# Changing the row format of all loads, the matmul tiling behind them and the whole instruction order of a retention and token-mixing kernel

## The chip, the cores and the metric

One core of a Trainium2 chip runs the whole program. The metric is the device time of one execution in microseconds, median over runs. A profile of one execution stands beside it; its times count from the first instruction of the span.

## What is computed

```python
# q, k, v: [4, 8, 768, 64] float32; w_q, w_k: [512, 64]; w_out: [512, 512]
gamma = 1 - 2.0 ** (-5 - arange(8))                 # one decay per head
for t in range(768):
    state = gamma * state + outer(k[t], v[t])       # per batch and head, 64x64
    y[t] = scale * q[t] @ state
x = y, heads side by side                           # [4, 768, 512]
W_tok = scale * (x @ w_q) @ (x @ w_k).T            # per batch, 768 x 768
mixed = W_tok @ x                                   # [4, 768, 512]
out = relu(mixed) @ w_out                           # [4, 768, 512] float32
```

The kernel multiplies in the other order: z = (x w_k)^T x, a 64 x 512 matrix for each batch, is summed over the tokens; then (x w_q) z is `mixed`. So a batch's z needs all of its 768 tokens.

## The kernel before, in words

The 3072 tokens are cut into 12 **pairs** of two chunks of 128 tokens, three pairs to a batch (NP = 3); pair p has 8 heads, held as 4 head pairs of 2 x 64 columns (HP = 4). Every step of every pair is a small function. Nothing is scheduled automatically: the list ORDER names the steps one after the other, with the engine of each copy or cast (`:A` is ScalarE, shown as ACT; `:V` VectorE, DVE; `:P` GpSimd, POOL) and the PSUM bank (`@2`). Each engine works through its own instructions in that order and waits where an input is missing.

The steps of pair p: `ck`, `cq`, `cv` cast k, q, v from the float32 staging tiles `k_st`, `q_st`, `v_st` to the bfloat16 tiles `ks`, `qs`, `vs` (cv also multiplies by the decay table `fv`). `trk`, `trq` transpose ks and qs on TensorE into PSUM (the PSUM tile is called `banks`), `ek`, `eq` (or `ekq`) copy the result out (`kq`). `sc` computes scores, `eat` masks them into `at_sb`; `st` adds k^T v to the running state, `es` copies the state out (`s_sb`); `ia`, `in`, `ic` build y in PSUM from scores and state; `ex` scales y into x (`x_nat`). `xt`, `exT` transpose x; `wqk` computes x w_k and x w_q, `ew` and `ewt` evict them (`wk_n`, `wqT`); `zm` adds the pair's part of z, `ez` evicts z after the third pair; `mx` computes `mixed`, `r` is the relu, `pj` the projection by w_out, `eo` the eviction into `o_st`. `fill` multiplies a tile of zeros (`warm`), with no result used.

`load` (L151) brings each of k, q, v of a pair as 128 partitions x 8 heads x 512 bytes, one row being two neighbouring tokens. The pairs 0 to 3 (TYPES "2") work in this layout directly, with matmuls on 64 rows. The pairs 4 to 11 (TYPES "1") rearrange k and v while casting: `ck1`, `cv1` (L556) move each quarter to other partitions, four instructions of 64 partitions x 512 for each tensor. LOADS is the order of the DMAs on the SP queue; a load waits until the staging tile 18 loads earlier has been cast (STAGES). Stores (`s0`, `s11/1`) come after all loads, in 2 KB rows.

Of the kernel before, what the change touches and what calls it, by code (L numbers as in the profile page):

```python
# [17 lines left out]
ekq.0.0:A ck.1:A fill.6@6 st.0.0 cq.1:V cv.1:P cv.2:P es.0.0:A sc.0.1@0 cv.3:P eat.0.1:V mask:P  # L18
ck.4.0:P ck.2:A ck.4.1:P fill.2@6 st.0.1 cv.4.0:P sc.0.0@2 trq.1@4 cv.4.1:P trk.1@4 WO.1:P
ekq.1.1:V ekq.1.0:V es.0.1:V cq.2:A ck.5.0:P fill.1@6 ia.0.1@0 WO.0:P in.0@0 fill.2@6 sc.1.0@4  # L20
eat.0.0:V fill.4@6 sc.1.1@2 st.1.0 eat.1.0:V es.1.0:A ia.0.0@0 cv.5.0:P trk.2@4 ic.0@0 trq.2@4
st.1.1 eat.1.1:V ekq.2.0:V W:A cv.5.1:P ekq.2.1:A ex.0:V fill.3@6 sc.2.0@4 sc.2.1@2 in.1@0
eat.2.0:V ia.1.1@0 ia.1.0@0 es.1.1:A ck.6.1:P xt.0@4 st.2.0 cv.6.1:P eat.2.1:V ic.1@0 exT.0:V
ia.2.1@2 ex.1:V ia.2.0@2 ck.3:A es.2.0:A trk.3@4 ic.2@2 in.2@2 ex.2:V cv.6.0:P cv.7.0:P cq.3:A
wqk.0@6 trq.3@4 ekq.3.1:A ekq.3.0:V xt.1@0 st.3.0 exT.1:V es.3.0:A xt.2@2 cq.4:A exT.2:V cv.7.1:P
sc.3.0@4 ew.0:V sc.3.1@0 wqk.1@2 wqk.2@3 eat.3.1:V ewt.1:A ew.1:A trq.4@0 eat.3.0:V trk.4@0
ck.8.0:P ewt.2:A ew.2:A st.3.1 ic.3@2 cq.8:P cv.8.0:P cv.8.1:P in.3@2 ia.3.0@2 ia.3.1@2 ek.4:V
zm.0.0@4 ewt.0:V eq.4:A es.3.1:A ex.3:V cv.9.1:P sc.4.0@0 sc.4.1@5 st.4.0 eat.4.0:V xt.3@2 exT.3:V
eat.4.1:V es.4.0:A zm.0.1@4 ez.0:A mx.0@0 ck.5.1:A cq.5:V in.4.1@2 cv.9.0:P wqk.3@4 r.0:A ewt.3:A
ew.3:A ia.4.0@2 ia.4.1@2 in.4.0@2 trk.5@5 mx.1@0 ex.4:V st.4.1 trq.5@5 ek.5:V r.1:A eq.5:V  # L30
ck.10.1:P pj.0.1@4 eo.0.1:A pj.0.0@0 sc.5.0@5 es.4.1:V xt.4@3 sc.5.1@1 cv.10.0:P st.5.0 eo.0.0:A
pj.1.0@0 eat.5.0:V ck.6.0:A eat.5.1:V pj.1.1@5 exT.4:A es.5.0:V ia.5.0@3 ia.5.1@3 in.5.1@3
in.5.0@3 eo.1.0:A mx.2@0 eo.1.1:A ck.11.1:P cq.6:V ex.5:V wqk.4@2 ew.4:V trq.6@5 trk.6@5 eq.6:V
r.2:A xt.5@0 ek.6:V ewt.4:A pj.2.1@3 pj.2.0@2 sc.6.0@5 ck.7.1:A exT.5:V sc.6.1@0 wqk.5@4 eo.2.1:A
zm.1.0@3 cq.7:V eat.6.0:V ew.5:V eat.6.1:V st.6.0 zm.1.1@3 eo.2.0:A ck.7.0:A trk.7@5 es.6.0:A
trq.7@5 ez.1:A st.6.1 ewt.5:A eq.7:V ek.7:V mx.3@2 ia.6.1@0 ia.6.0@0 es.6.1:A st.7.0 r.3:A
in.6.1@0 es.7.0:A ex.6:V sc.7.0@5 mx.4@2 pj.3.1@4 r.4:A sc.7.1@0 eat.7.0:V pj.3.0@2 st.7.1 xt.6@5
eat.7.1:V exT.6:V ck.8.1:A eo.3.1:A pj.4.0@3 eo.3.0:A ia.7.1@1 es.7.1:A trq.8@5 cq.11:P in.7.0@1
ck.9.1:V trk.8@5 eo.4.0:A mx.5@3 in.7.1@1 eq.8:V ck.9.0:A ia.7.0@1 pj.4.1@0 r.5:A eo.4.1:A ek.8:V
sc.8.0@5 sc.8.1@3 cq.9:A st.8.0 ex.7:V es.8.0:A xt.7@1 exT.7:A pj.5.0@0 eat.8.1:V trq.9@3 trk.9@3  # L40
in.8.1@1 eo.5.0:A eat.8.0:V ek.9:V eq.9:A cv.10.1:P in.8.0@1 ia.8.1@1 cv.11.0:P ia.8.0@1 pj.5.1@0
ex.8:V wqk.6@6 xt.8@1 ew.6:V eo.5.1:A sc.9.1@3 cq.10:A exT.8:V wqk.7@0 wqk.8@1 ew.7:A zm.2.0@2
ck.10.0:A eat.9.1:V sc.9.0@3 ew.8:V ewt.6:A zm.2.1@2 st.9.0 ewt.8:A ez.2:A trk.10@5 trq.10@5
mx.6@1 eat.9.0:V es.9.0:A st.9.1 ewt.7:A in.9.1@3 r.6:A ek.10:V ia.9.0@3 ia.9.1@3 mx.7@0 eq.10:V
es.9.1:A ex.9:V ck.11.0:A r.7:A sc.10.0@5 eat.10.0:V st.10.0 pj.6.0@2 trk.11@3 trq.11@3 eq.11:V
ek.11:V eo.6.0:A sc.10.1@0 es.10.0:A xt.9@5 eat.10.1:V pj.6.1@2 in.10.0@3 cv.11.1:P in.10.1@3
exT.9:A sc.11.0@5 eo.6.1:A st.10.1 es.10.1:A eat.11.0:V wqk.9@2 ia.10.1@3 ia.10.0@3 ew.9:A ewt.9:A
sc.11.1@0 ex.10:V mx.8@5 eat.11.1:V st.11.0 r.8:A pj.7.1@2 in.11.0@3 xt.10@5 exT.10:V es.11.0:A
in.11.1@3 ia.11.0@3 ia.11.1@3 pj.8.0@0 ex.11:V wqk.10@1 eo.7.1:A xt.11@3 ewt.10:V exT.11:V ew.10:A
eo.8.0:A pj.7.0@6 wqk.11@3 ew.11:V eo.7.0:A zm.3.0@0 ewt.11:V zm.3.1@0 ez.3:A mx.11@0 r.11:A  # L50
mx.10@3 mx.9@5 pj.8.1@2 pj.11.1@0 eo.8.1:A pj.11.0@1 eo.11.1:A r.10:V r.9:A pj.10.0@2 pj.10.1@0
eo.10.0:A eo.11.0:V eo.10.1:A pj.9.1@6 eo.9.1:A pj.9.0@2 eo.9.0:A
# [5 lines left out]
q10 v10 k11 q11 v11 s0 s1 s2 s3 s4 s5 s6 s7 s8 s11/1 s11/0 s10/0 s10/1 s9/1 s9/0  # L58
""".split()

TYPES = "222211111111"
STAGES = 18
OBUFS = 11
CASTS = dict(k=6, v=6, q=4)
WBYTES = 512
OBYTES = 2048
KQS = 2
# [3 lines left out]
def kernel(  # L71
# [35 lines left out]

# [16 lines left out]
    def bank32(b, n=1):  # L124
        return banks[:, b : b + n, :].rearrange("p n f -> p (n f)")
# [4 lines left out]
    pairs = [dict() for _ in range(NG)]  # L130
    z_sbs = [None] * B
# [9 lines left out]

    def load(name, p, half=None, eng=None):
        src = {"k": k, "q": q, "v": v}[name]
        b, cp = divmod(p, NP)
        st = pairs[p]
        if name + "_st" not in st:
            st[name + "_st"] = stage_pool.tile([128, 2, HP, 2, D], FP32, name=name + "_st", tag="st")
        xs = slice(0, 2) if half is None else slice(half, half + 1)  # L150
        dma = (eng or nc.sync).dma_start(  # L151
            out=st[name + "_st"][:, xs].rearrange("g x hp j d -> g (x hp) (j d)"),
            in_=src[b, xs.start * HP : xs.stop * HP, cp * 2 * C : (cp + 1) * 2 * C, :].rearrange(
                "h (g j) d -> g h (j d)", j=2
            ),
        )
    wstages = {}

    def load_weights(token):
        w_st = stage_pool.tile([128, 2, HP, 2, D], FP32, name=token + "_st", tag="st").rearrange(  # L160
            "p x hp j d -> p (x hp j d)"
        )
        if token == "w":
            st = w_st[:, 0 : 2 * NDM * DH].rearrange("p (w a h) -> p w a h", w=2, a=NDM)
            for i, src in enumerate((moe_w_q, moe_w_k)):
                nc.sync.dma_start(out=st[:, i], in_=src.rearrange("(a p) h -> p a h", p=128))
        else:
            st = w_st.rearrange("p (a m) -> p a m", a=2)
            for i in range(2):
                a = 2 * int(token[1:]) + i  # L170
                nc.sync.dma_start(
                    out=st[:, i], in_=moe_w_out[128 * a : 128 * a + 128, :], max_dma_last_dim=WBYTES
                )
        wstages[token] = st

    def load_token(token):
        if token[0] in "wo":
            load_weights(token)
        else:
            load(token[0], int(token[1:]))  # L180

    load("k", 0, 0, nc.scalar)
    load("k", 0, 1, nc.sync)

    queue = list(LOADS)
    staged = ["k0"]
    cast = set()

    def more_loads():
        while queue:
            token = queue[0]
            if token[0] == "s":
                if not stored(token[1:]):
                    return
                queue.pop(0)
                continue
            n = len(staged)
            if n >= STAGES and staged[n - STAGES] not in cast:  # L200
                return
            staged.append(token)
            load_token(queue.pop(0))

    parts = {}

    def release(token, n):
# [8 lines left out]

    warm = const_pool.tile([128, 512], BF16, name="warm")
    nc.vector.memset(warm, 0.0)  # L218


    ln_v = const_pool.tile([128, NP, H, 2], FP32, name="ln_v")
    ln_y = const_pool.tile([128, NP * 2, H], FP32, name="ln_y")
    for h in range(H):
        ln = math.log(1.0 - 2.0 ** (-5.0 - h))
        nc.vector.memset(ln_v[:, :, h, :], -ln)
        nc.vector.memset(ln_y[:, :, h], ln)
    tv = const_pool.tile([128, NP, H, 2], FP32, name="tv")
    nc.gpsimd.iota(
# [688 lines left out]
```

## Time and profile before

| | |
|---|---|
| median of 3 runs | 101.49 us (99.64, 101.49, 101.58) |
| span of the profiled execution | 98.4 us, first to last instruction |
| busy TensorE / DVE / ACT / POOL | 85.4 / 72.4 / 64.4 / 59.8 us |
| moved by DMA | 20.19 MB read, 6.29 MB written, 26.74 MB in all queues |
| DMA rate, mean over the span | 272 GB/s |

The profiled execution has no time of its own beside the span; the median of the runs lies 3.1 us above the span, which is start and end of the program outside of it. The page cuts the span into 40 slices of 2.46 us: busy tenths of each engine, the granted TensorE clock (PEclk, 9 is full), the mean busy share of the 16 DMA engines and GB/s. Views by time list instructions with start and duration; TensorE matmuls are pipelined, so the distance from the start of one group to that of the next says what a group costs, and the duration says more than that.

### The profile page before, as it was taken

The numbers are of one execution on the slowest core, as the hardware profiler recorded it, in microseconds if no ns is written. First come the engines' busy times: TensorE is split into PE (matmuls) and PEld (weight loads), VectorE is DVE, ScalarE is ACT, GpSimd is POOL, SyncE is SP. The second block draws the span as 40 slices with busy tenths as digits, with TensorE's granted clock in tenths as the row PEclk, the third lists the DMA queues.
The fourth block names the chain that finished last, engine by engine and source line by source line (L and its number), as shares of the span: only waits on it lengthen the run. The fifth ranks groups of instructions, "written<-read, shape, count | busy, mean of one in ns | idle before, by whom it ended". The sixth has DMA issues, their size and how long they took to land. (4 is left out here: it accounts for less than half of the span.)

```text
span 98.4 us, 4214 instructions
## 1 busy us (share of the span) xinstructions
PE 85.4 (87%) x1847; PEld 54.9 (56%) x1861; DVE 72.4 (74%) x105; ACT 64.4 (65%) x110; POOL 59.8 (61%) x77
## 2 busy tenths in 40 slices
PE   4999789876697988999999999689999999989950
PEld 1334465564585775655747647357786576644410
DVE  3032489999489299979999899998899999624200
ACT  4344823928090458969799899987899955347750
POOL 4646070250989998999999999999999800000000
PEclk9999999999955699999999999999999999999999
DMA  1999998999999999999999999999998150040983
GB/s 18 291 347 347 339 343 200 308 295 309 314 335 316 301 271 286 333 320 316 315 330 318 272 307 295 336 327 341 394 401 321 37 214 9 0 191 22 388 340 125
DMA packets 43954, 26.74 MB, mean 272 GB/s; under 512 B 1952, under 2 KB 40864, under 8 KB 43936
## 3 DMA queue, kind: packets, MB, share of 16 engines
q1 hardware_dynamic: 43408, 26.22, 86.1%
q8 instruction: 14, 0.23, 0.9%
q10 hardware_dynamic: 528, 0.26, 0.9%
q14 instruction: 4, 0.03, 0.1%
HBM read 20.19 MB, written 6.29 MB: 269 GB/s over the span
## 5 line engine op out<-in xcount | busy, mean ns | idle before, releaser
L556 POOL TENSOR_TENSOR vs<-v_st,fv 64x512 bf16<-64x512 f32 x32 | 34.8, 1086 | 2.2 <-DMA v_st<-in_v_dram 0.2
L831 PE MATMUL banks<-wout_sb,relu 128*128 128x512 bf16 x85 | 21.7, 380 | 1.0 <-issue 0.6
L639 DVE TENSOR_TENSOR at_sb<-banks,cmask 128x1024 bf16<-128x1024 f32 x16 | 19.1, 1217 | 1.1 <-PE banks L627 1.1
L136 ACT CAST ks<-k_st 64x512 bf16<-64x512 f32 (+2 forms) x20 | 13.6, 682 | 5.9 <-DMA k_st<-in_k_dram 5.6
L362 POOL TENSOR_TENSOR vs<-v_st,fv 128x1024 bf16<-128x1024 f32 (+1 forms) x4 | 7.2, 1810 | 13.2 <-DMA v_st<-in_v_dram 13.2
L136 ACT COPY o_st<-banks 128x512 f32<-128x512 f32 x23 | 13.2, 587 | 2.7 <-PE banks L831 2.5
L137 DVE COPY kq<-banks 128x1024 bf16<-128x1024 bf16 x18 | 11.8, 686 | 2.5 <-PE banks L585 1.8
L831 PEld LDWEIGHTS <-relu 128*128 128x128 bf16 x96 | 8.2, 98 | 8.8 <-issue 0.4
L824 ACT ACTIVATE relu<-banks 128x1024 bf16<-128x1024 f32 x11 | 11.3, 1024 | 2.1 <-PE banks L809 1.6
L328 PE MATMUL banks<-warm 128*128 128x512 bf16 x34 | 11.0, 467 | 1.6 <-DVE warm L218 1.3
L136 ACT COPY kq<-banks 128x1024 bf16<-128x1024 bf16 x6 | 6.0, 1011 | 6.5 <-PE banks L386 4.6
L712 DVE TENSOR_TENSOR x_nat<-banks,fy 128x1024 bf16<-128x1024 f32 x8 | 9.8, 1220 | 0.6 <-PE banks L664 0.3
L429 DVE TENSOR_TENSOR at_sb<-banks,cmask 128x1024 bf16<-128x1024 f32 x8 | 9.4, 1216 | 0.4 <-PE banks L417 0.2
L137 POOL CAST ks<-k_st 64x512 bf16<-64x512 f32 x14 | 8.5, 608 | 0.8
L758 PE MATMUL banks<-xT,wqk_w 128*128 128x256 bf16 x48 | 8.1, 297 | 0.0
L136 ACT CAST qs<-q_st 128x1024 bf16<-128x1024 f32 (+1 forms) x6 | 5.9, 979 | 2.9 <-DMA q_st<-in_q_dram 2.9
L136 ACT CAST s_sb<-banks 128x256 bf16<-128x256 f32 x17 | 6.4, 377 | 1.2 <-PE banks L678 1.0
L328 PEld LDWEIGHTS <-warm 128*128 128x128 bf16 x37 | 3.7, 114 | 6.1 <-issue 3.2
L627 PE MATMUL banks<-kq 64*128 64x128 bf16 x128 | 5.9, 217 | 1.1 <-DVE kq L137 0.8
L137 DVE CAST qs<-q_st 128x1024 bf16<-128x1024 f32 (+1 forms) x5 | 4.2, 850 | 3.3 <-DMA q_st<-in_q_dram 3.3
L137 DVE COPY xT<-banks 128x1024 bf16<-128x1024 bf16 x9 | 6.2, 685 | 0.3 <-PE banks L730 0.3
L530 DVE TENSOR_TENSOR x_nat<-banks,fy 128x1024 bf16<-128x1024 f32 x4 | 4.9, 1218 | 1.7 <-PE banks L461 1.6
(78 smaller groups left out, 134.6 us busy)
## 6 DMA issues: line engine op xcount, KB each, us to landing
q_st<-in_q_dram SPq DMA_DIRECT2D x12, 512.0 KB, 6.6
v_st<-in_v_dram SPq DMA_DIRECT2D x12, 512.0 KB, 6.5
k_st<-in_k_dram SPq DMA_DIRECT2D x11, 512.0 KB, 6.4
out_dram<-o_st SPq DMA_DIRECT2D x9, 512.0 KB, 6.4
out_dram<-o_st SPq DMA_DIRECT2D x6, 256.0 KB, 2.0
o_st<-in_moe_w_out_dram SPq DMA_DIRECT2D x4, 256.0 KB, 5.2
k_st<-in_k_dram ACTq DMA_DIRECT2D x1, 256.0 KB, 4.2
k_st<-in_k_dram SPq DMA_DIRECT2D x1, 256.0 KB, 3.9
```

What stands on the lines that cost most here:

```text
L136: return nc.scalar.copy(out=out, in_=in_)
L137: return ENGINES[e].tensor_copy(out=out, in_=in_)
L328: nc.tensor.matmul(out=bank32(b), lhsT=warm[:, 0:128], rhs=warm, start=True, stop=True)
L362: ENGINES[e].tensor_tensor(out=st["vs"][:, :, :, xs].rearrange("p hp j x d -> p x (hp j) d"), in0=st["v_st"][:, xs].rearrange("p x hp j d ...
L429: ENGINES[e].tensor_tensor(out=st["at", half].rearrange("p x hi j t -> p (x hi) (j t)"), in0=st["at_ps", half].rearrange("p (n t) -> p n t ...
L556: ENGINES[e].tensor_tensor(out=st["vs"][rows(j), c].rearrange("p hp x d -> p x hp d"), in0=st["v_st"][rows(c), :, :, j], in1=fv[rows(c), p ...
L627: nc.tensor.matmul(out=ps[:, x, hi, c, :], lhsT=st["kT"][rows(x), hp, c, :], rhs=st["qT"][rows(x), hp, c, :], start=(hi == 0 and c == 0), ...
L639: ENGINES[e].tensor_tensor(out=st["at", half].rearrange("p x hi c t -> p (x hi c) t"), in0=st["at_ps", half].rearrange("p (n t) -> p n t", ...
L712: nc.vector.tensor_tensor(out=st["x"].rearrange("p x c i n -> p (x c i n)").rearrange("p (m d) -> p m d", d=D), in0=st["y_ps"].rearrange(" ...
L758: nc.tensor.matmul(out=st["wq_ps"], lhsT=wqk_sb[:, a, 0 : 2 * DH], rhs=st["xT"][:, a].rearrange("p c t -> p (c t)"), start=False, stop=(a ...
L824: nc.scalar.activation(out=dst, in_=st["mx_ps"], func=ACT.Relu)
L831: nc.tensor.matmul(out=bank32(b), lhsT=st["relu"][:, a, j, :], rhs=wout_sb[:, a, :], start=(a == 0), stop=(a == NDM - 1),)
```

## The change

All pairs get one type, "3". A k or v row is one token of one head, 256 bytes, and a partition is a token: two DMAs of 128 x 8 x 64 for each load, so that casts are one whole instruction of 128 x 1024 (`cast`). A q row is 8 neighbouring tokens, 2 KB; the transposes of q undo this order with a permuted identity, `perm`. w_out comes in 2 KB rows instead of 512 bytes. `wqk` becomes `wk` and `wq`: wq is computed for the two chunks in two column tiles (64 output rows each), and both results stand side by side in PSUM, so that `ew` evicts them in one instruction (`w_sb`). z is put on both row halves (`ez` in three parts), `mx` runs by 128 columns on the row half of its chunk, `r` is one relu of 128 x 512 for each chunk. Transposes may go to one bank, 8 of 128 x 128 (`@4`), or two banks, 16 of 64 x 64 (`@12`). The order of all steps, of loads and of stores is new, with 14 fill matmuls, all at the start, instead of 37 spread over the first third. Stage tiles are 17.

```diff
-ck.0.0:V ck.0.1:A fill.15@6 trk.0@0 cq.0.1:A cq.0.0:V fill.4@6 trq.0@0 cv.0.1:P cv.0.0:V ekq.0.1:A
...
+fill.14@6 mask.3:P ck.0.0:A ck.0.1:P cq.0:A trk.0@0 trq.0@12 ek.0:V cv.0.0:P eq.0:V sc.0.0@12
...
-q0 v0 k1 q1 v1 k2 q2 w v2 k3 q3 v3 k4 q4 v4 o0 o1 k5 q5 v5 k6 q6 v6 k7 q7 v7 k8 q8 v8 k9 q9 v9 k10
...
+k0 q0 v0 q1 k1 k2 q2 v1 w v2 k3 q3 q4 k4 v3 v4 q5 o1 o0 k5 q6 k6 v5 v6 q7 k7 v7 k8 q8 k9 q9 v8 k10
+v9 k11 q11 q10 v10 v11 s0/0 s2/1 s0/1 s1/1 s2/0 s1/0 s3/1 s4/1 s4/0 s3/0 s5/0 s5/1 s8/0 s6/1 s8/1
...
-TYPES = "222211111111"
-STAGES = 18
+TYPES = '333333333333'
+STAGES = 17
...
+            if name == "q":
+                t = st.rearrange("p (x e) -> p x e", x=2)
+                nc.sync.dma_start(
+                    out=t,
+                    in_=src.rearrange("(h x) (g j) d -> g h x (j d)", x=2, j=J),
+                )
...
+                t = st.rearrange("p (c h d) -> p c h d", c=2, h=H)
+                for c in range(2):
+                    nc.sync.dma_start(
+                        out=t[:, c], in_=src[:, c * C : (c + 1) * C].rearrange("h p d -> p h d")
+                    )
...
+    def wq(e, bs, p):
...
+        for a in range(NA):
+            for c in range(2):
+                nc.tensor.matmul(
+                    out=st["w_ps"][rows(c), 1],
+                    lhsT=wq_w[:, a, :],
+                    rhs=st["xT"][:, a, c, :],
...
+    def mx(e, bs, p):
...
+                nc.tensor.matmul(
+                    out=st["m_ps"][c][:, a * C : a * C + C],
+                    lhsT=z[rows(c), half ^ c, i * C : i * C + C],
+                    rhs=st["w"][rows(c), 1, :],
...
+    def r(e, bs, p, c):
+        st = pairs[p]
+        st["r", c] = relu_pool.tile([128, NA, C], BF16, name="relu")
```

What stands first on the SP queue before (after its half of k0; the other half is on ACT's queue): one DMA for each of k, q, v.

```order
L151 DMA k_st<-in_k_dram 128x4x128
L151 DMA q_st<-in_q_dram 128x8x128
L151 DMA v_st<-in_v_dram 128x8x128
L151 DMA k_st<-in_k_dram 128x8x128
L151 DMA q_st<-in_q_dram 128x8x128
L151 DMA v_st<-in_v_dram 128x8x128
```

What stands first there after the change, where the last number of a row counts the elements of a DMA row (64 of float32 are 256 bytes, 512 are 2 KB):

```order
L189 DMA k_st<-in_k_dram 128x8x64 x2
L177 DMA q_st<-in_q_dram 128x2x512
L189 DMA v_st<-in_v_dram 128x8x64 x2
L177 DMA q_st<-in_q_dram 128x2x512
L189 DMA k_st<-in_k_dram 128x8x64 x4
L177 DMA q_st<-in_q_dram 128x2x512
L189 DMA v_st<-in_v_dram 128x8x64 x2
L162 DMA w_st<-in_moe_w_q_dram 128x4x64
L162 DMA w_st<-in_moe_w_k_dram 128x4x64
```

Each k or v has become two DMAs, all on SP; q1 has moved ahead of k1, and k2 and q2 ahead of v1.

The last casts on POOL before, those of pairs 8 to 11 (each v in four instructions of 64 x 512):

```order
L137 CAST ks<-k_st 64x2x4x64 x2
L137 CAST qs<-q_st 128x2x8x64
L556 TENSOR_TENSOR vs<-v_st,fv 64x2x4x64 x8
L137 CAST ks<-k_st 64x2x4x64 x2
L556 TENSOR_TENSOR vs<-v_st,fv 64x2x4x64 x2
L137 CAST ks<-k_st 64x2x4x64 x2
L137 CAST qs<-q_st 128x2x8x64
L556 TENSOR_TENSOR vs<-v_st,fv 64x2x4x64 x6
```

The last casts on POOL after it, from k10 on; the rows with `vs` are v9, v10 and the two halves of v11:

```order
L146 CAST ks<-k_st 128x1024
L402 TENSOR_TENSOR vs<-v_st,fv_169 128x1024
L146 CAST ks<-k_st 128x512 x2
L146 CAST qs<-q_st 128x2x8x64 x2
L402 TENSOR_TENSOR vs<-v_st,fv_169 128x1024
L402 TENSOR_TENSOR vs<-v_st,fv_169 128x512 x2
```

POOL now casts k, q and v of the last pairs, in the order in which they are loaded, and v11 is the last thing that it does.

More of the change, by code (lines that the diff above doesn't have):

```diff
@@ L23 @@
[L23 to L34, printed above, removed]
@@ L157 @@
[L157 to L174, printed above, removed]
@@ L185, with store @@
+    def store(p, c):
+        b, cp = divmod(p, NP)
+        t0 = cp * 2 * C + c * C
+        nc.sync.dma_start(
+            out=out[b, t0 : t0 + C, :], in_=pairs[p]["o"][:, c], max_dma_last_dim=2048
+        )
     queue = list(LOADS)
-    staged = ["k0"]
-    cast = set()
+    staged = []
+    done = set()
+    parts = {}
     def more_loads():
@@ L194, in more_loads, with release @@
             if token[0] == "s":
-                if not stored(token[1:]):
+                p, _, cs = token[1:].partition("/")
+                cs = [int(cs)] if cs else [0, 1]
+                if not all(("o", int(p), c) in done for c in cs):
                     return
[L197 to L207, printed above, removed]
+                for c in cs:
+                    store(int(p), c)
+            else:
+                n = len(staged)
+                if n >= STAGES and staged[n - STAGES] not in done:
+                    return
+                staged.append(token)
+                load(token)
+            queue.pop(0)
+    def release(token, n=1):
         parts[token] = parts.get(token, 0) + 1
         if parts[token] == n:
-            cast.add(token)
+            done.add(token)
             more_loads()
@@ new lines @@
+    for x in range(2):
+        nc.vector.tensor_tensor(
+            out=ty[:, :, x],
+            in0=ty[:, :, x],
+            in1=lng.rearrange("p (h x) -> p x h", x=2)[:, x][:, None, None, :].to_broadcast(
+                [128, NP, 2, HP]
+            ),
+            op=ALU.mult,
+        )
+    nc.scalar.activation(out=fy, in_=ty, func=ACT.Exp)
+    nc.vector.tensor_copy(
+        out=perm.rearrange("p (c h g) -> p c h g", c=2, h=4),
+        in_=identity.rearrange("p (c g h) -> p c h g", c=2, h=4),
+    )
@@ new lines, with W @@
+    wout_sb = const_pool.tile([128, NA, DM], BF16, name="wout_sb")
+    def W(e, b):
+        st = zs[0]["w_st"]
+        copy(e, wq_w, st[:, 0])
+        for a in range(NA):
+            dst = wk_w[:, a].rearrange("p (j g) -> p j g", j=J)
+            src = st[:, 1, a].rearrange("p (g j) -> p j g", j=J)
+            if e == "A":
+                nc.scalar.mul(out=dst, in_=src, mul=float(wk_scale))
+            else:
+                ENGINES[e].tensor_scalar_mul(out=dst, in0=src, scalar1=float(wk_scale))
+        release("w")
@@ new lines, in WO, with fill, cast, step @@
+    def WO(e, b, i):
+        copy(e, wout_sb[:, 2 * i : 2 * i + 2], zs[i]["o_st"])
+        release(f"o{i}")
+    def fill(e, b, n):
+        for _ in range(n):
+            nc.tensor.matmul(
+                out=banks[:, b[0], :], lhsT=warm[:, 0:128], rhs=warm, start=True, stop=True
+            )
+    def cast(name, pl):
+        def step(e, b, p, c=None):
+            st = pairs[p]
+            if name + "s" not in st:
+                st[name + "s"] = pl.tile([128, 2, H, D], BF16, name=name + "s")
+            dst, src, cp = st[name + "s"], st[name + "_st"], p % NP
+            if TYPES[p] == "3":
+                cs = slice(0, 2) if c is None else slice(c, c + 1)
+                o = dst[:, cs].rearrange("p c h d -> p (c h) d")
+                i = src[:, cs].rearrange("p c h d -> p (c h) d")
+                f = fv3[:, 2 * cp + cs.start : 2 * cp + cs.stop].rearrange("p c h -> p (c h)")
+                todo = [(o, i, f)]
+            else:
+                todo = [
+                    (dst[rows(j), i], src[rows(i), :, j * D : j * D + D], fv1[rows(i), cp, :, j])
+                    for i in ((0, 1) if c is None else (c,))
+                    for j in range(2)
+                ]
+            for o, i, f in todo:
+                if name == "k":
+                    copy(e, o, i)
+                else:
+                    ENGINES[e].tensor_tensor(
+                        out=o, in0=i, in1=f.to_broadcast(list(o.shape)), op=ALU.mult
+                    )
+            release(name + str(p), 1 if c is None else 2)
+        return step
@@ L320, in W @@
-        release("w", 1)
-    def WO(e, b, i):
-        copy(e, wout_sb[:, 2 * i : 2 * i + 2], wstages[f"o{i}"])
-        release(f"o{i}", 1)
-    def fill(n, b):
-        for _ in range(n):
-            nc.tensor.matmul(
-                out=bank32(b), lhsT=warm[:, 0:128], rhs=warm, start=True, stop=True
-            )
-    def halves(half):
-        return slice(0, 2) if half is None else slice(half, half + 1)
-    def cast_kq(e, p, name, half):
-        st = pairs[p]
-        if name + "s" not in st:
-            st[name + "s"] = cast_pool.tile([128, HP, 2, 2, D], BF16, name=name + "s", bufs=CASTS[name])
-        xs = halves(half)
-        copy(
-            e,
-            st[name + "s"][:, :, :, xs].rearrange("p hp j x d -> p x (hp j) d"),
-            st[name + "_st"][:, xs].rearrange("p x hp j d -> p x (hp j) d"),
-        )
-        release(name + str(p), 1 if half is None else 2)
@@ L552, in cv1, with sc @@
+    def sc(e, bs, p, half):
         st = pairs[p]
[L553 to L563 removed]
@@ L623, in sc1 @@
+        st["at_ps", half] = two(sorted(bs))
         for hi in range(2):
@@ L815, in mx, with ez @@
+                    start=(cp == 0 and c == 0),
+                    stop=(cp == NP - 1 and c == 1),
                     skip_group_check=True,
                 )
-        st["mx_ps"] = bank32(b, 2)
-    def r(e, b, p):
-        st = pairs[p]
-        st["relu"] = relu_pool.tile([128, NDM, 2, C], BF16, name="relu")
-        dst = st["relu"].rearrange("p a j t -> p (a j t)")
+    def ez(e, bs, bt, part):
+        if part == 0:
+            zs[bt]["z"] = z_pool.tile([128, 2, 2 * C], BF16, name="z_sb")
+            copy(e, zs[bt]["z"][:, 0], zs[bt]["ps"])
+        else:
+            c = part - 1
+            copy(e, zs[bt]["z"][rows(c), 1], zs[bt]["ps"][rows(1 - c)])
```

840 lines of the change are left out of this document (318 added, 522 removed).

## The prediction

> **What bounds the kernel now.** I read the 40 slices first, for what is full and when.
>
> ```profile
> PE   4999789876697988999999999689999999989950
> PEclk9999999999955699999999999999999999999999
> DMA  1999998999999999999999999999998150040983
> GB/s 18 291 347 347 339 343 200 308 295 309 314 335 316 301 271 286 333 320 316 315 330 318 272 307 295 336 327 341 394 401 321 37 214 9 0 191 22 388 340 125
> ```
>
> The DMA engines are full from slice 1 to about slice 30; after that only stores are left. TensorE has holes in the first third, a stretch at a half clock from slice 11 to 13, and is full from slice 15 to the end. So I cut the program at the first `mx` (L809), the end of the first third, and count what TensorE still has to do there. In TensorE's timeline, each row is a group: start, duration, line, operation, number of instructions.
>
> ```profile
> 37.85 0.39 PE L809 MATMUL banks<-wqT,z_sb 64*128 64x256 bf16 x4 [0.47 <-ACT z_sb L136]
> ...
> 51.53 0.41 PE L749 MATMUL banks<-wqk_w,xT 128*128 128x64 bf16 x8
> 51.77 0.60 PE L758 MATMUL banks<-xT,wqk_w 128*128 128x256 bf16 x4
> 52.30 0.63 PE L790 MATMUL banks<-x_nat,wk_n 128*64 128x256 bf16 x8
> 52.76 0.29 PE L678 MATMUL banks<-vs,ks 128*64 128x64 bf16 x8
> ...
> 53.23 0.41 PE L585 MATMUL banks<-identity,ks 64*128 64x64 bf16 x16
> 53.47 0.40 PE L605 MATMUL banks<-identity,qs 64*128 64x64 bf16 x16
> 53.80 0.32 PE L678 MATMUL banks<-vs,ks 128*64 128x64 bf16 x8
> 54.05 0.39 PE L809 MATMUL banks<-wqT,z_sb 64*128 64x256 bf16 x4
> 54.37 0.64 PE L698 MATMUL banks<-vs,at_sb 128*128 128x64 bf16 x16
> 54.94 0.32 PE L678 MATMUL banks<-vs,ks 128*64 128x64 bf16 x8
> 55.19 0.29 PE L664 MATMUL banks<-s_sb,kq 64*128 64x64 bf16 x8
> 55.32 0.39 PE L627 MATMUL banks<-kq 64*128 64x128 bf16 x8
> 55.62 0.39 PE L809 MATMUL banks<-wqT,z_sb 64*128 64x256 bf16 x4
> ...
> 88.77 5.99 PE L831 MATMUL banks<-wout_sb,relu 128*128 128x512 bf16 x27 [0.16 <-issue]
> ```
>
> The distance to the next start is what a step costs: 16 transposes 0.24 and 0.33 (I take 0.28), `st` 0.25, `mx` 0.32, `ia` 0.57 for two, `in` 0.13, `sc` 0.30, the wk part of `wqk` 0.24 and its wq part 0.53, `zm` 0.46 for two. The last row holds the seven `pj` of the end, 0.86 each. ORDER lists behind the first `mx`: 24 pj (20.6), 22 transposes (6.2), 12 mx (3.8), 14 sc (4.2), 12 st (3.0), 14 in (1.8), 16 ia (4.6), 9 wqk (6.9), 9 zm (2.1): 53.2 us. TensorE took 94.76 − 37.85 = 56.9 for it, **1.07 times the sum**. So the last 57 us are TensorE work with 7% of small waits, and the first 38 us are something else: loads, the half clock and latency.
>
> **What follows TensorE, and the copy engines.** After the last projection there is one eviction and one store.
>
> ```profile
> 94.80 0.59 ACT L136 COPY o_st<-banks 128x512 f32<-128x512 f32 x1 [0.28 <-PE banks L831]
> ```
>
> ```profile
> 0.00:37.85 37.85, 31.45 (x771) 20.37 (x775) 24.65 (x48) 18.21 (x31) 21.59 (x39) 0.91 0.99 287
> 37.85:95.40 57.55, 53.94 (x1077) 34.49 (x1088) 47.75 (x58) 46.19 (x80) 38.22 (x39) 1.00 0.83 267
> ```
>
> The first row gives 0.6 us, and 98.4 − 95.4 leaves 3.0 us for the store: 3.6 together. The two rows of the stages (length, then busy time of TensorE, its weight loads, DVE, ACT, POOL, granted clock, DMA share, GB/s) show DVE and ACT at four fifths of the second stage, which is below TensorE.
>
> **Loads, the part that changes most.** No load of 256-byte rows of k or v is in the trace, but w_q and w_k are read in such rows. Their issues and the last load's, the median times from issue to landing (last number of a row), and the rates in quarters of a microsecond:
>
> ```profile
> 11.08 1.40 SPq L166 DMA_DIRECT2D w_st<-in_moe_w_q_dram  x1
> 12.52 0.94 SPq L166 DMA_DIRECT2D w_st<-in_moe_w_k_dram  x1
> ...
> 62.40 2.39 SPq L151 DMA_DIRECT2D v_st<-in_v_dram  x1
> ```
>
> ```profile
> v_st<-in_v_dram SPq DMA_DIRECT2D x12, 512.0 KB, 6.5
> ...
> w_st<-in_moe_w_q_dram SPq DMA_DIRECT2D x1, 128.0 KB, 6.0
> w_st<-in_moe_w_k_dram SPq DMA_DIRECT2D x1, 128.0 KB, 5.1
> ```
>
> ```profile
> 12.25:12.50 0.25, 0.25 (x29) 0.25 (x21) 0.25 (x1) 0.00 (x0) 0.00 (x0) 1.00 1.15 348
> ...
> 15.00:15.25 0.25, 0.25 (x6) 0.13 (x3) 0.25 (x1) 0.20 (x1) 0.00 (x0) 1.00 1.25 289
> 15.25:15.50 0.25, 0.25 (x3) 0.13 (x2) 0.25 (x1) 0.00 (x0) 0.00 (x0) 1.00 1.22 279
> 15.50:15.75 0.25, 0.25 (x3) 0.02 (x1) 0.25 (x1) 0.00 (x0) 0.00 (x0) 1.00 1.00 229
> 15.75:16.00 0.25, 0.25 (x2) 0.05 (x1) 0.25 (x2) 0.00 (x0) 0.00 (x0) 1.00 0.55 130
> 16.00:16.25 0.25, 0.18 (x13) 0.21 (x16) 0.25 (x2) 0.00 (x0) 0.00 (x0) 1.00 0.42 79
> ```
>
> w_q and w_k land at 17.1 and 17.6, so their rows pass in the 2 us before. In the quarters from 15 us, at full share (the column before the last), 279 GB/s pass, where 512-byte rows make 348. Then comes a hole, with the engines half idle. Either the hole is one late engine at the seam of two DMAs, and 279 is the rate; or it belongs to the short rows, and the mean of the five quarters, 201 GB/s, is. I take **279**, because the share is full there and the hole shows idle engines, and keep 201 and 348 as the ends. For 2 KB rows the trace has only stores: 394 and 401 GB/s in slices 28 and 29, mean 398, which I take for loads of q and w_out; the other end is 347.
>
> k and v are 12.58 MB: 45.1 us. q is 6.29 MB: 15.8; w_out 1.05 MB: 2.6; w 0.26 MB: 0.9. Together 64.5 us at full flow. Before, slices 2 to 5 run at 344 GB/s and slices 7 to 27 at 312 on average, a loss of 10%. A part of that is SP waiting for staging tiles:
>
> ```profile
> SPq L151 <- POOL vs L556: 5.2, 5, 1.9
> ```
>
> and more for other casts. After the change a tile is needed again 17 loads later, some 30 us, and I expect no such wait; I take a loss of 8%: 69.7 us. Flow starts at about 2.4 (slice 0 is empty), so **v11 lands at 72.1**. Before, it is issued at 62.4 and lands at 68.9: the loads end later now, not earlier.
>
> The Trainium skill (DMA: Bandwidth & Descriptors, Why small descriptors are slow) counts 3 cycles of overhead for each packet beside one for 32 bytes, thus 11 cycles for 256 bytes against 19 for 512; from 344 GB/s that is an estimate of 297, and v11 would land 3 us sooner. The same page (Specifications) wants 512 bytes and more for line rate, with a read-modify-write below: that speaks for the low end and against this change.
>
> **From v11 to the end.** POOL casts v10 whole and v11 in halves.
>
> ```profile
> L556 POOL TENSOR_TENSOR vs<-v_st,fv 64x512 bf16<-64x512 f32 x32 | 34.8, 1086 | 2.2 <-DMA v_st<-in_v_dram 0.2
> ...
> L362 POOL TENSOR_TENSOR vs<-v_st,fv 128x1024 bf16<-128x1024 f32 x3 | 5.7, 1901 | 11.2 <-DMA v_st<-in_v_dram 11.2
> ```
>
> v10 lands one v (1.9 us at 279 GB/s) before v11, and takes 1.9; so v11's halves are done 1.9 us after its landing, at 74.0. Behind that cast stand 4 ia, 4 in, 5 mx, 12 pj, 2 xt, 2 wk, 2 wq and 3 zm on TensorE: 15.9 us by the prices above, with wq at 0.27 (half of the row, for two column tiles side by side; if they do not overlap it is 0.53, and the sum 0.5 more). Times 1.07: 16.9. With 3.6 behind: 74.0 + 16.9 + 3.6 = **94.5**.
>
> **From the first mx, for the same end.** The new order puts it behind v4 and q5. By the same rates the loads up to v4 take 26.3 us, 28.4 with loss, so v4 lands at 30.8; its cast follows at 32.7, and ten steps of TensorE (2.6 us) and about 1 us of copies follow that: the first mx at 36.3, against 37.85. Behind it: 24 pj, 12 mx, 14 sc, 12 st and 9 zm as before; 17 transposes in two banks (4.8) and 5 in one bank (8 of full rows; between the 0.24 of a row above and twice that, 0.43 taken as nearer to no overlap: 2.2); 13 in, 14 ia, 9 wk, 9 wq (2.4 against 4.8). Sum 50.9, times 1.07 is 54.4. 36.3 + 54.4 + 3.6 = **94.3**, the same end.
>
> **The rest, off the path.** POOL loses 32 × 1.09 = 34.8 us and gains 8 × 1.9 = 15.2 of whole v casts, then takes over casts of k and q; it stays below the loads, which hide it. `ew` in one instruction saves 12 evictions; z in three parts adds 8, and relu by chunk costs more starts: about level, hidden by TensorE as long as ACT and DVE have their fifth of slack; without it they would cost 2 or 3 us. The 23 fill matmuls that go ran in holes and free nothing.
>
> **The sum.** Two paths end together, and TensorE's queue has to follow both: where a load is late, steps behind it that could run wait too. I add 1 us to the later: span 95.5. The median of the runs stands 3.1 above the profiled span, so the time is **98.6**.
>
> **Rivals.**
> (a) Copies and TensorE run with less friction, because no cast is in quarters: factor 1.03 in place of 1.07, and short rows at the 289 GB/s of the first quarter. First mx at 35.5, then 52.4 and 3.6: span 91.5, by the loads 92, time 94.5 to 95. For: POOL was full from 36 to 78. Against: the waits in the second stage are few already.
> (b) The half clock. It came at slices 11 to 13, where TensorE was least busy; without the fills TensorE has 15 us of work in the first 36, counted in the same way, so it may stay there longer. Each slice at half clock with TensorE full costs 1.2 us; three to five more of them cost 3.6 to 6: time 102 to 105. The Trainium skill (TensorE: Matmul & The Clock Gate, Part 1) has the clock halved after an idle window and back after a busy one of about 3.4 us; the seven microseconds here agree with two such windows.
> (c) **Slower**: the hole is the rate of short rows. At 201 GB/s k and v take 62.6, all loads 82.3 (the loss is in the rate), v11 lands at 84.7, the end is 84.7 + 1.9 + 16.9 + 3.6 = 107.1, time 110.2. By the sum with its loss of 8% it is level with before at 258 GB/s for k and v, and 2% slower at 248: a rate little below 279 decides. For: the hole follows the short rows. Against: the share is low in it. The Trainium skill's 512-byte rule, named above, leads here.
> (d) The new order does nothing: first mx at 37.9 and a pace of 1.1, because evictions in more pieces wait more: 97.5, time 100.6.
>
> **Chances.** Forecast 0.50 (own range 96 to 101), (a) 0.16, (b) 0.14, (c) 0.13, (d) 0.07. Two per cent, about what a measurement of this kernel can tell from none, is 99.5 and 103.5. Faster: two thirds of the forecast and (a), 0.50. Slower: (c) and a part of (b), 0.17. Same: 0.33. The range 94 to 106 leaves out the far part of (c) and a little of (a).
>
> **What would show it.** GB/s in the profile after, in slices 4 to 25: 255 to 280 with a full share if the rate is right, 200 to 230 in (c). v11's issue ends near 68 to 70. The first `mx` near 36 and 91 at the end of TensorE; waits of TensorE for casts of v8 to v11 if the loads decide. PEclk tells (b). Wrong would make it: an order of the loads in which some other tensor than v11 is late, or evictions that wait for each other, with ACT full.

## The result, and the profile after

The changed kernel takes **149.5 us** (median of 4 runs, 148.9 to 151.9) against 101.5 for the kernel before: a ratio of 1.485, 95% interval 1.469 to 1.500. The forecast was 98.6, its range 94 to 106. The profiled execution has a span of 147.9 us. Some executions of a kernel run at a lower clock and take longer; the medians here are over all executions, the ratios and intervals over the undisturbed ones alone, which is why 102.2 us can stand beside a ratio of 1.000 further down.

The 40 slices of the page after, 3.7 us each, in the lines that were read first of before:

```profile
PE   6954646794369997495549667249376875679990
PEclk9999555579655599999975859955855775859999
DMA  4999899999999899999999921201100000213175
```

The loads are over with slice 22, at 85 us: 13 later than forecast, and yet not the reason, for 63 us follow in which nothing is full for long but TensorE at the very end. While the loads run, TensorE stands between 3 and 7 tenths in 16 of 23 slices, and the clock falls to half beside that. Something makes it wait in the middle of its own work. TensorE's and DVE's timelines show what, at one place (the number in brackets is the idle time ahead of the row, and what ended it):

```profile
94.84 0.40 PE L482 MATMUL banks<-qT,kT 64*128 64x128 bf16 x8 [2.37 <-DVE at_sb L494]
95.18 0.41 PE L555 MATMUL banks<-vs,at_sb 128*128 128x64 bf16 x8
98.03 0.59 PE L687 MATMUL banks<-wout_sb,relu 128*128 128x512 bf16 x1 [2.44 <-DVE at_sb L494]
```

```profile
93.57 1.23 DVE L494 TENSOR_TENSOR at_sb<-banks,mask 128x1024 bf16<-128x1024 f32 x1 [3.56 <-ACT kT L145]
95.62 1.23 DVE L568 TENSOR_TENSOR x_sb<-banks,fy 128x1024 bf16<-128x1024 f32 x1 [0.83 <-PE banks L555]
96.76 1.22 DVE L494 TENSOR_TENSOR at_sb<-banks,mask 128x1024 bf16<-128x1024 f32 x1
```

L687 is `pj`: it reads `relu` and w_out and needs nothing of `at_sb`. It starts at 98.03, when the masking of scores that began at 96.76 ends at 97.98. In ORDER this place reads

```
sc.9.1@16 ia.8.0@04 ex.8:V eat.9.1:V pj.5.0@3
```

`eat.9.1` reads the scores in banks 1 and 6; `pj.5.0` writes bank 3. They share no data and no bank. But the pair is read by one instruction, as one strided access (`banks[:, lo:hi+1:hi-lo, :]` in the function `two`), and bank 3 lies between 1 and 6. The kernel before has neighbours alone (`b : b + 2`); after the change 40 of 60 pairs are apart. I traced every semaphore wait that stands in the two built programs back to the instruction that it waits for. After the change, by my count, 34 waits between a copy and TensorE, and 25 between DVE and ACT, join instructions that have no bank in common, where one's banks only lie in the other's stretch from lo to hi. Before there is none of either.

**Theory (the envelope):** a copy of two banks that are apart is ordered against all work in the banks between. **Rivals:** the new order has too much latency in its true dependences; the short rows; the half clock for want of fills.

### The profile page after: what moved, and what is told of

Its sections match the earlier page's. It is cut to its first block, busy times and chain, and to the rows that moved or that the text cites. A ratio compares the mean times of both kernels' runs of the same rounds, so it can differ in the third digit from the quotient of the medians.

```text
span 147.9 us, 3782 instructions
## 1 busy us (share of the span) xinstructions
PE 100.1 (68%) x1620; PEld 68.4 (46%) x1630; DVE 66.5 (45%) x92; ACT 63.5 (43%) x107; POOL 45.1 (30%) x46
## 5 line engine op out<-in xcount | busy, mean ns | idle before, releaser
L494 DVE TENSOR_TENSOR at_sb<-banks,mask 128x1024 bf16<-128x1024 f32 x24 | 29.0, 1222 | 25.4 <-PE banks L482 8.4
L687 PE MATMUL banks<-wout_sb,relu 128*128 128x512 bf16 x86 | 27.2, 445 | 7.4 <-DVE at_sb L494 2.4
L402 POOL TENSOR_TENSOR vs<-v_st,fv 128x1024 bf16<-128x1024 f32 (+1 forms) x14 | 23.1, 1657 | 12.5 <-DMA v_st<-in_v_dram 9.9
L568 DVE TENSOR_TENSOR x_sb<-banks,fy 128x1024 bf16<-128x1024 f32 x12 | 14.7, 1225 | 16.8 <-PE banks L555 9.8
L145 ACT COPY o_sb<-banks 128x512 f32<-128x512 f32 x20 | 11.7, 587 | 18.6 <-PE banks L687 18.6
L482 PE MATMUL banks<-qT,kT 64*128 64x128 bf16 x192 | 11.3, 249 | 10.5 <-DVE at_sb L494 4.7
L687 PEld LDWEIGHTS <-relu 128*128 128x128 bf16 x96 | 9.9, 111 | 17.9 <-issue 11.7
L146 POOL CAST qs<-q_st 128x1024 bf16<-128x1024 f32 x9 | 9.4, 1041 | 18.7 <-DMA q_st<-in_q_dram 13.3
L555 PE MATMUL banks<-vs,at_sb 128*128 128x64 bf16 x192 | 12.1, 224 | 3.5 <-DVE at_sb L494 1.7
L679 ACT ACTIVATE relu<-banks 128x512 bf16<-128x512 f32 x18 | 10.3, 600 | 6.2 <-PE banks L665 4.8
L555 PEld LDWEIGHTS <-at_sb 128*128 128x128 bf16 x192 | 9.6, 117 | 5.8 <-issue 4.4
L146 POOL CAST ks<-k_st 128x1024 bf16<-128x1024 f32 (+1 forms) x10 | 9.1, 912 | 8.3 <-DMA k_st<-in_k_dram 7.5
```

What stands on the lines that cost most here:

```text
L145: return nc.scalar.copy(out=out, in_=in_)
L146: return ENGINES[e].tensor_copy(out=out, in_=in_)
L402: ENGINES[e].tensor_tensor(out=o, in0=i, in1=f.to_broadcast(list(o.shape)), op=ALU.mult)
L482: nc.tensor.matmul(out=ps[:, x, hi, c, :], lhsT=st["kT"][rows(x), hp, c, :], rhs=st["qT"][rows(x), c, hp, :], start=(hi == 0 and c == 0), ...
L494: ENGINES[e].tensor_tensor(out=st["at", half].rearrange("p x hi c t -> p x (hi c) t"), in0=st["at_ps", half].rearrange("p x (n t) -> p x n ...
L555: nc.tensor.matmul(out=y[:, x, c, hp, :], lhsT=st["at", half][:, x, hi, c, :], rhs=st["vs"][:, c, 2 * hp + x, :], start=first(p, x), stop= ...
```

## Experiments: the bank pairs

**e1_split.** Each such copy in two pieces, here `eat`; `ex`, `ek`, `eq`, `exT` likewise:

```diff
+    def split(bs):
+        if abs(bs[0] - bs[1]) == 1:
+            return [slice(0, 2)]
+        return [slice(0, 1), slice(1, 2)]
...
+        for i in split(st["at_bs", half]):
+            ENGINES[e].tensor_tensor(
+                out=st["at", half].rearrange("p x hi c t -> p x (hi c) t")[:, i],
+                in0=st["at_ps", half].rearrange("p x (n t) -> p x n t", t=C)[:, i],
```

> The changed kernel; every copy that reads two PSUM banks that are not neighbours (40 of them: eat, ex, ek, eq, exT) is cut into two instructions, one for each bank. Order, banks and loads stay. Theory of the envelope: an instruction that reads banks 1 and 6 as one strided access is ordered against all that happens in banks 2 to 5, by semaphore waits that nothing in the data asks for; in the program there are 34 such waits between a copy and TensorE and 25 between DVE and ACT, and none after the cut. It expects a fall from 149.5 to 100-112, with 40 more copies as the price. Rival, latency of the new order: 145-153, since every true dependence is left. Rival, short rows: 145-153, the loads are the same. Rival, half clock for want of fill matmuls: 140-153, the fills are still gone.

**e2_renamed.** Banks renamed throughout ORDER, at the place above for example:

```diff
-sc.9.1@16 ia.8.0@04 ex.8:V eat.9.1:V pj.5.0@3
+sc.9.1@01 ia.8.0@56 ex.8:V eat.9.1:V pj.5.0@2
```

> The changed kernel with the numbers behind @ in ORDER renamed, so that each pair of banks is a pair of neighbours (0 of 60 pairs apart, before the renaming 40); no instruction is added, none moves. Envelope: 96-107, a little below the kernel with the cut copies. Latency of the order: 143-153, a little less because the banks come free in another order. Short rows: 145-153. Half clock: 140-153.

**e3_before_far.** The kernel before with `BANK = [0, 3, 6, 2, 5, 1, 4, 7]` and each pair read as in `two`:

```diff
-        return banks[:, b : b + n, :].rearrange("p n f -> p (n f)")
+        lo, hi = sorted((BANK[b], BANK[b + 1]))
+        return banks[:, lo : hi + 1 : hi - lo, :]
```

> The kernel before with its banks renamed by 0 3 6 2 5 1 4, so that no pair is one of neighbours and each two-bank copy is one strided access; instructions, order and loads are those of before. It gets 67 waits between copies and TensorE that nothing in the data asks for. Envelope: slower than before, 115-155. Every rival: 101.5, within 2%, since order, rows and fills are those of before.

Measured: e1 **108.7** (ratio to before 1.073, 1.049 to 1.097), e2 **110.3** (1.089, 1.058 to 1.120), e3 **180.4** (177.5 to 181.4, against 101.4 for before). Cutting or renaming alone takes 39 to 41 us away; renaming and reading the pairs as one strided access adds 79 to the kernel before. Every rival expected no change in at least one of them, and falls as the main cause. Two sizes were missed: e2 lies above the 96 to 107 that the theory gave it, which the next part takes up, and e3 above its 115 to 155. Whether e1 or e2 is faster cannot be told, as their intervals overlap. The same place with renamed banks, TensorE and then DVE:

```profile
73.72 0.41 PE L554 MATMUL banks<-vs,at_sb 128*128 128x64 bf16 x8
74.18 0.81 PE L686 MATMUL banks<-wout_sb,relu 128*128 128x512 bf16 x3
```

```profile
74.24 1.22 DVE L567 TENSOR_TENSOR x_sb<-banks,fy 128x1024 bf16<-128x1024 f32 x1 [2.36 <-PE banks L554]
75.38 1.21 DVE L493 TENSOR_TENSOR at_sb<-banks,mask 128x1024 bf16<-128x1024 f32 x1
```

`pj` now starts 1.2 us ahead of the masking that it stood behind. The strided access itself costs nothing: the masking in groups by form, in the kernel before, after the change, and then in the kernel before with banks apart:

```profile
L639 DVE TENSOR_TENSOR at_sb<-banks,cmask 128x1024 bf16<-128x1024 f32 x16 | 19.1, 1217 | 1.1 <-PE banks L627 1.1
```

```profile
L494 DVE TENSOR_TENSOR at_sb<-banks,mask 128x1024 bf16<-128x1024 f32 x24 | 29.0, 1222 | 25.4 <-PE banks L482 8.4 <-ACT s_sb L145 6.2 <-ACT kT L145 3.6
```

```profile
L645 DVE TENSOR_TENSOR at_sb<-banks,cmask 128x1024 bf16<-128x1024 f32 x16 | 19.5, 1222 | 22.7 <-PE banks L633 10.0 <-ACT o_st L142 2.7 <-PE banks L736 2.5
```

All take 1217 to 1222 ns, with neighbours alone in the first and none in the last; what grows is the idle time ahead (1.1, then 25.4 and 22.7 us). The half clock follows the waits: with renamed banks the clock is 0.936 on average against 0.767 in the changed kernel, with the fills still gone, and in the kernel before, which keeps its fills, it falls from 0.965 to 0.693 when the banks are put apart. The page of the kernel before with banks apart shows the same picture as that of the changed kernel:

```profile
PE   7956556478555959648356777729833766777761
PEclk9999855555555587987955555555895558559998
```

## Experiments: the short rows

**e4_rows512.** In the kernel with renamed banks; the values of k and v lie in other places then, so its output is not the wanted one and only its time is used:

```diff
-                for c in range(2):
-                        out=t[:, c], in_=src[:, c * C : (c + 1) * C].rearrange("h p d -> p h d")
+                for i in range(2):
+                        out=u[:, i],
+                        in_=src[i * HP : (i + 1) * HP].rearrange("h (g j) d -> g h (j d)", j=2),
```

> The kernel with renamed banks, its loads of k and v made in 512-byte rows, two DMAs of 256 KB each as with the short ones; the values then lie in other places of the staging tile, so the result is another one, but every instruction on the engines is the same. Envelope: the short rows cost at most what the loads end later, so 0-7 us less than with renamed banks, and 93-103. Short rows as the main cause: 15 us or more less than with renamed banks. Latency or half clock as the main cause: no change against renamed banks, within 2%.

**e5_rates**, and **e11_rates_2q** (v on ACT's queue in the first part), **e12_rates_seams** (four DMAs a tile in the first part, then two beside q on ACT's queue): loads without compute.

> Loads alone, no compute: all k and v in 256-byte rows (12.58 MB, two DMAs of 256 KB for each tile), then the same in 512-byte rows, then all q in 2 KB rows, all into the 17 staging tiles without casts; at the end 24 stores of zeros. The outputs are not computed. The forecast counted 279 GB/s for the short rows: 45 us. Rival (c) counted 201: 63 us. With 512-byte rows I expect 340 to 350 (36-37 us), with 2 KB rows 398 (15.8 us) in the forecast, and not under 347. If the short rows run at 265 or more here, the late loads in the kernel with renamed banks (end near 83) come from something else than the rows, such as SP waiting for staging tiles.

> Loads alone as before, but in the first part (256-byte rows) k is issued by SP and v by ACT, on two queues. With one queue the short rows ran at 240 GB/s on average, and 512-byte rows at 343. If the rate of short rows is set by what each packet takes at the DMA engines: 235-245 again. If holes at the seams of DMAs of one queue cost it: 260-290. The outputs are not computed.

> Loads alone: first all k and v in 256-byte rows in four DMAs of 128 KB a tile (before: two of 256 KB) on one queue, then again in two DMAs of 256 KB, with the 12 loads of q on ACT's queue at the same time; then 24 stores. If the loss lies at the seams of DMAs of one queue, twice as many seams cost more: 190-215 GB/s in the first part against 240, and above 300 with q beside them. If it lies in the packets alone: 240 again in the first part. The outputs are not computed.

Measured: e4 **102.2** (1.000, 0.990 to 1.010): the short rows cost 8 to 9 us (8.1 between the medians, 1.089 against 1.000 in the ratios). That is beyond the 0 to 7 that the envelope theory expected, and little more than half of what they would need as the main cause. POOL's last row, for e2 the second half of v11, for e4 v10 and both halves of v11 (start, duration):

```profile
83.65 1.05 POOL L401 TENSOR_TENSOR vs<-v_st,fv 128x512 bf16<-128x512 f32 x1 [0.16 <-DMA v_st<-in_v_dram]
```

```profile
65.25 3.90 POOL L403 TENSOR_TENSOR vs<-v_st,fv 128x1024 bf16<-128x1024 f32 x3 [1.69 <-DMA v_st<-in_v_dram]
```

The casts end at 84.7 and at 69.2. The rates (last column) of e5 in 256-byte, 512-byte and 2 KB rows, then of the short rows in e11, then of e12 in smaller DMAs and beside q:

```profile
2.00:52.00 50.00, 0.00 (x0) 0.00 (x0) 1.00 1.05 237
54.00:89.00 35.00, 0.00 (x0) 0.00 (x0) 1.00 1.12 334
92.00:99.00 7.00, 0.00 (x0) 0.00 (x0) 1.00 1.06 398
```

```profile
3.00:44.00 41.00, 0.00 (x0) 0.00 (x0) 1.00 1.28 288
```

```profile
5.00:55.00 50.00, 0.00 (x0) 0.00 (x0) 1.00 1.03 231
70.00:118.00 48.00, 0.00 (x0) 0.00 (x0) 1.00 0.98 247
```

Short rows run at 237 GB/s on one queue, neither at the 279 that the forecast took nor at rival (c)'s 201, and at 288 with k and v on two queues. DMAs of half the size slow them by 3% only (231), and q beside them lifts next to nothing (247 in all, where I expected above 300): the seams of DMAs are not most of the loss. Why two queues of short rows bring 288 stays open.

**e13_renamed_q2, e14_q_on_act, e15_v_on_act**: can the second queue give the 8 us back?

```diff
-                nc.sync.dma_start(
+                nc.scalar.dma_start(
```

A new step in ORDER (`lq` in e13, `go` in e14 and e15) names the place in ACT's order at which such a load may go out.

> The kernel with renamed banks (110.3), its loads of q issued by ACT on a second queue, each at a place in ACT's order near the time at which SP issued it; nothing else moves. If a second queue fills the holes, k and v run near 280 while q passes and the loads end 5 to 8 us sooner: 102-106, towards the 102.2 of 512-byte rows. If ACT's issue blocks its copies, or q takes its share from k and v that are needed first: 108-112.

> The kernel with renamed banks, q loaded by ACT on its own queue, each load at its place in LOADS' order (LOADS halts at a q until ACT's order has reached it). In the load of 8 DMAs before a q no wait is left that is longer than a transfer. If the second queue fills what one queue leaves idle: 104-108 against 110.3. If ACT's stream is held by its own loads: 110-118.

> The same with v, all in 256-byte rows, on ACT's queue, and k and q on SP's; 24 loads on ACT at about 0.6 us each, so ACT gets 14 us more work on top of 63. If two queues bring 288 GB/s as in the loads alone: loads end near 72 and the time is 102-107. If ACT's 14 us and its waits weigh more: 110-120.

Measured: **127.9** (1.269, 1.256 to 1.283), **110.2** (1.081, 1.071 to 1.092), **114.6** (1.126, 1.115 to 1.137). No. In e13, whose loads of q stand late in the program, a copy engine waited behind its own load for a DMA of v, and POOL for q, by the list of waits:

```profile
POOL qs L145 <- DMA q_st<-in_q_dram: 39.6, 5, 15.9
ACT qs L144 <- DMA v_st<-in_v_dram: 14.1, 1, 14.1
```

In e15 the rate does rise, to 300 GB/s from 10 to 70 us, against 253 with renamed banks alone:

```profile
10.00:70.00 60.00, 45.77 (x972) 33.62 (x976) 41.80 (x50) 31.59 (x52) 36.68 (x30) 0.86 1.15 300
```

```profile
10.00:70.00 60.00, 46.30 (x1005) 34.16 (x1007) 41.86 (x49) 35.19 (x57) 31.55 (x24) 0.89 1.02 253
```

but each load then stands in ACT's line of copies, that of v11 last, and copies wait behind it, a relu for 4.1 us:

```profile
69.92 2.12 ACTq L188 DMA_DIRECT2D v_st<-in_v_dram  x2
```

```profile
ACT relu L685 <- DMA v_st<-in_v_dram: 4.1, 1, 4.1
```

The cast of v11 ends at 77.9 there, 6.8 sooner than with renamed banks alone, and TensorE still goes on until 109.8, 6.1 later. In e14 the cast ends at 82.8 and TensorE at 104.8: the loads gain 1.9 us and the end gains nothing. How much each wait takes of this was not separated.

**e7_mix, e8_all512** (`TYPES = '131313131313'` and all `'1'` in the renamed kernel): longer rows with the casts that go with them.

> The kernel with renamed banks; pairs 0, 2, 4 to 10 take k and v in 512-byte rows and cast them in quarters as the kernel before did, the others stay with 256-byte rows and whole casts. POOL and ACT get 23 us more of casts (quarter casts 4 x 1.09 for v in place of 1.9; 4 x 0.62 for k in place of 1.05), the loads end some 6 us sooner. If the rows decide: 103-107 against 110 with short rows alone. If the casts decide: 109-114.

> The kernel with renamed banks, every pair with 512-byte rows and quarter casts. The loads end near 70, but POOL gets some 44 us more (45 to about 89). If the rows decide: 101-104. If the casts decide, POOL's 89 us are the bound with 19 us of TensorE and 3.6 behind: 108-115.

Measured: **108.8** (1.076, 1.064 to 1.088), just under the 109 that I expected at least if the casts decide, and **119.1** (1.184, 1.174 to 1.193), above the 115 at most. Rows and casts are one trade: with quarter casts everywhere the loads are early, but POOL casts almost without a pause until 95.0 us, and its last row, v10 and v11, is:

```profile
86.17 8.82 POOL L401 TENSOR_TENSOR vs<-v_st,fv 64x512 bf16<-64x512 f32 x8
```

## Experiments: the matmul part alone

**e6_before_col**: wq in column tiles, z on both halves, `mx` in 8 pieces, in the kernel before. **e9_before_col_z**: z's three copies on one engine. **e10_before_col_w**: also one eviction for wk and wq.

```diff
+        copy(e, z_sbs[bt][:, 0], z_ps)
+        copy("V", z_sbs[bt][rows(0), 1], z_ps[rows(1)])
+        copy(e, z_sbs[bt][rows(1), 1], z_ps[rows(0)])
```

> The kernel before with one part of the change alone: wq as two column tiles side by side, z on both row halves in three copies, mx by 8 matmuls of 128 columns (each chunk its own bank), ewt as a plain copy. Rows, casts, banks and order stay. If the second stage is TensorE work, as the forecast says, 9 wq of 0.53 us become 0.27 and it ends 2.4 us sooner: 98.5-100. If the z copies on ACT and DVE cost what it saves, 100.5-102.5. If wq's column tiles do not overlap, nothing is gained and the copies add up to 2: 101.5-103.5.

> As the kernel before with wq in column tiles and z on both halves, but all three copies of z of a batch on one engine (ACT, ACT, ACT) in place of ACT, DVE, ACT. There mx waited 5.1 us for z's last copy, which waited 3.8 us for DVE's. If the change of engines on one bank is what made it slow: 101-103.5 (what is left are two more copies of 0.37 ahead of each mx). If it is the column tiles, the mx in 8 pieces or the permuted relu: 105-107, no change.

> The same, and wk and wq evicted by one copy of 256 columns in place of two (the changed kernel's w_sb). ACT and DVE make 12 copies less and mx no longer waits for the second one: 1-3 us less than with z on one engine alone, 98.5-102. If evictions are hidden, no change against it.

Measured: **106.6** (1.057, 1.048 to 1.066), **104.8** (1.035, 1.021 to 1.048), **104.1** (1.038, 1.031 to 1.044). The part that I had counted as a gain of 2.4 us costs. In e6's waits, `mx` (L810) stands behind the third copy of z, and that one behind DVE's: in this program two engines that read one bank wait for each other, though the second and third copies read different rows.

```profile
PE banks L810 <- ACT z_sb L136: 5.1, 5, 2.2
ACT z_sb L136 <- DVE z_sb L137: 3.8, 4, 2.0
```

One engine for z gives a part back; the single eviction brings nothing that the intervals can tell. And TensorE's busy time behind 38 us did not fall: 54.7 in e10, against 53.9 in the row of before.

```profile
38.00:99.00 61.00, 54.73 (x1189) 36.01 (x1200) 48.55 (x58) 48.22 (x83) 37.89 (x39) 1.00 0.78 252
```

`mx` still waits for z in e10, 3.0 us by its list of waits against 0.9 in the kernel before; what else makes up the remaining 3.8% I did not separate. No kernel tried here beats the one before.

## Why the prediction was wrong, by its own steps

**The step that failed** is the factor of 1.07 for small waits in "From v11 to the end" and "From the first mx". It was measured on the old order and laid on the new one, whose instructions are priced there but not the banks in which they stand. The working read `@12` and `@4` as two or one bank, never looked at pairs such as `@16`, and so had no term for the 39 us (149.5 − 110.3) which are four fifths of the slowdown of 48. In the changed kernel these rows end the casts of v10 and v11 on POOL and the work of TensorE:

```profile
82.80 3.90 POOL L402 TENSOR_TENSOR vs<-v_st,fv 128x1024 bf16<-128x1024 f32 x3
```

```profile
138.08 6.22 PE L687 MATMUL banks<-wout_sb,relu 128*128 128x512 bf16 x27
```

From 86.7 to 144.3 are 57.6 us, where the forecast had 16.9. Its last line came near ("evictions that wait for each other"), but with ACT full, and ACT is busy 43% of the span. None of its rivals held this mechanism; (c) was the slower one, and that its 110.2 is what remains once the waits are gone is luck in part, as its terms show.

**The loads.** The step that chose 279 over 201 failed: the short rows make 237 on one queue. With 237 in the forecast's own sum, k and v take 53.1 us instead of 45.1, all loads 72.4, with the loss of 8% 78.2, and v11 lands at 80.6 instead of 72.1; in e2 its cast ends at 84.7 where the forecast had 74.0, so the loss was larger too. What the hole in the trace of before was, from which 279 and 201 were read, no run shows. Nor was the wait for staging tiles gone, which the forecast had put at nothing; in e2 SP waits for casts of k before loads of k and v (in all, times, longest):

```profile
SPq L188 <- POOL ks L145: 3.8, 2, 2.0
```

From the cast of v11 on, e2 follows the load path of the forecast:

```profile
97.45 6.22 PE L686 MATMUL banks<-wout_sb,relu 128*128 128x512 bf16 x27
```

TensorE ends at 103.7, 19.0 us after the cast (forecast 16.9), and the span at 107.3, 3.6 behind (forecast 3.6). Rival (c)'s span of 107.1 came from a rate that is too low and a loss that is missing: right in the sum, not in its terms. The Trainium skill (DMA: Bandwidth & Descriptors, Specifications) wants 512 bytes or more for line rate; 334 against 237 GB/s agrees that rows below are slower, but 512 bytes are not the full rate here, as 398 with 2 KB shows. From the Trainium skill (the same page, Why small descriptors are slow) came the estimate of 297 GB/s; the 288 on two queues are near it, the 237 on one are not.

**The pace.** e4 has neither the envelope nor the short rows and still takes 102.2, not 98.6; its ratio of 1.000 says that it is level with before. Its first `mx`, and the stage from there to the end of TensorE:

```profile
37.01 0.22 PE L666 MATMUL banks<-w_sb,z_sb 64*128 64x128 bf16 x1
```

```profile
37.01:96.20 59.19, 53.60 (x1106) 35.94 (x1112) 40.41 (x46) 43.90 (x80) 24.75 (x20) 1.00 0.75 248
```

The first `mx` came at 37.0 (forecast 36.3). Behind it TensorE took 59.2 us, to 96.2, for the work priced at 50.9: a factor of 1.16 at full clock, not the 1.07 carried over from before. So even without its two faults the new order is no faster than the old; rival (d), with a factor of 1.1 and 100.6, was nearest. Two things make 1.16 of 1.07. TensorE is busy for 53.6 us there, against 53.9 in the second stage of before, so the 2.3 us that the cheaper matmuls should have saved (53.2 to 50.9) do not show in its busy time. And it idles for 5.6 us in place of 3.0 (56.9 − 53.9). Why the busy time did not fall stays open.

**From span to time.** The 3.1 us that were added came from the span of one execution and the median of others. On record each execution takes 1.6 to 2.8 us more than its own span, mostly 1.7 (109.0 against 107.3 in e2), so some 1.4 us of the 98.6 had no ground; it is a small error beside the others.

**What held:** single prices on TensorE. In e2 a wq in column tiles takes 0.25 us (80.97 to the next start at 81.22; forecast 0.27) and a transpose in one bank 0.46 (79.85 to 80.31; forecast 0.43):

```profile
79.85 0.62 PE L431 MATMUL banks<-perm,qs 128*128 128x128 bf16 x8
80.31 0.40 PE L598 MATMUL banks<-wk_w,xT 128*128 128x64 bf16 x8
...
80.97 0.41 PE L612 MATMUL banks<-xT,wq_w 128*64 128x128 bf16 x8
81.22 0.29 PE L507 MATMUL banks<-vs,ks 128*64 128x64 bf16 x8
```

But a price that falls on TensorE is no gain where copies ahead of it grow, as e6 shows. Rival (b) had cause and effect the wrong way round here: most of the half clock came with the waits. With renamed banks it is left in slices 5 to 9 of 40; what that costs, no run separates.

## What to carry to other kernels

When an order or an allocation is rewritten, read the buffer numbers as closely as the instructions: ask of every access whether its stretch, first to last element, covers buffers in which others work, and compare the waits of the two programs, not only the instructions. If one instruction must read two buffers, make them neighbours; renaming adds no instruction here and was worth 39 us. And take a factor for small waits from an order only for that order.

## What the runs showed of the hardware

The rate of loads by row, 237, 334 and 398 GB/s for 256, 512 and 2048 bytes on one queue, is set for 256 bytes by more than the bytes: two queues bring 288, DMAs of half the size 231. The masking copy takes the same 1217 to 1222 ns whether its two PSUM banks are neighbours or not.
